# Sliding-window attention ahead of a routed network: the last half block of 64 keys goes into the fourth block's tile, padded with zeros to 128 rows

## The chip, the cores and the metric

The kernel runs on one core of one Trainium2 chip. The metric is device time in microseconds (us) of one execution; several executions are timed and the median is given. The five engines of the core are named as in the profile: PE (matrix multiplication; its loading of weights is listed apart as PEld), DVE (vector), ACT (scalar, activation functions), POOL (GpSimd) and SP, which here only issues DMAs. They run at the same time and wait for one another through semaphores; each works through its own list of instructions in order.

## What is computed

The first part is attention with a sliding window, for 8 batches, 8 heads, 576 positions and 64 values a head:

```python
scores = scale * np.matmul(q, k.transpose(0, 1, 3, 2))
rel = pos[:, None] - pos[None, :]
slopes = 2.0 ** (-8.0 * (np.arange(H) + 1) / H)
bias = slopes[:, None, None] * (-np.abs(rel))[None, :, :]
mask = (rel >= 0) & (rel < 128)
scores = np.where(mask, scores + bias[None], -1000000000.0)
attn = softmax(scores)            # over the keys
out = np.matmul(attn, v)
```

The outputs of the heads are put side by side into a token's 512 values, 4608 tokens in all. The second part is a network of 8 experts, every token through every expert:

```python
P = np.exp(x @ w_gate - max)
for _ in range(8):                # rows and columns in turn
    P /= P.sum(1, keepdims=True) + 1e-09
    P /= P.sum(0, keepdims=True) + 1e-09
    P *= N / E
for e in range(E):
    out += P[:, e:e+1] * (np.maximum(x @ w1[e], 0.0) @ w2[e])
```

The change lies in the attention alone.

## The kernel before

**Tiling of the attention.** A batch's 576 positions are cut into four blocks of 128 and a half block of 64 (`SM` = 512, `TL` = 64, `NKB` = 5 blocks). A query sees only keys of its own block and of the block before it. So a step `(b, kb, u)` takes batch `b`, key block `kb` and one half of the heads (`u` = 0 or 1, four heads each). Scores are made transposed, keys on the partitions and queries along the row, so that they can be the stationary operand of the product with v without another transpose.

- `scores` (L407) multiplies block `kb` of the keys with the queries of blocks `kb` and `kb + 1`. Each head has 64 values, so its operands lie on 64 partitions; two heads (`hb` = 0 and 1) lie on partitions 0 to 63 and 64 to 127 and are issued as a pair. Blocks 0 to 2 give 128 by 256 scores a head in one matmul (L416). Block 3 takes two: 128 queries of its own (L416) and the 64 of the half block (L423), 192 columns in all. Block 4 is the half block: 64 keys by 64 queries (L416).
- `exps` (L430) lets ACT take the exponential of the four heads' scores from PSUM into the tile `pt`; `masks` (L442) lets DVE multiply `pt` with a precomputed `mask`, which holds the position bias as a factor and zero outside the window. The mask of a head has 256 columns: own block, next block. `make_mask` (L237) has ACT write it once, at the start.
- `values` (L453) multiplies, for each head, `pt` of the block before and of the own block with v (65 columns: 64 values and a column of ones, which gives the sum of the weights) into one PSUM tile `psN`, eight matmuls of 128 by 128 by 65. For block 4 these are four matmuls with 128 rows and 64 columns, then four of 64 by 64 (L469 puts them in that order). DVE divides by the sums (L482, L483) into `xsb`.
- `turn_x` (L500) transposes `xsb` for the second part, through PE in batches 0 to 2 and 7 and through a DMA in batches 3 to 6, and stores it to DRAM through SP (`xd`, L498).

**The half block's q and k.** `load_tail` brings 64 rows of q and 64 of k of all heads; transposed, they stand in the tile `TT` (`homes`, L295), 64 columns of queries and 64 of keys. In batches 0 to 2 PE transposes them and ACT copies them there (L364), in later batches a DMA does it (`turn_tail`, L321). v comes in by `load_v`, and POOL casts it to 16 bits (`cast_v`, L384), with a small clearing that writes the column of ones (L389).

**The order of the work.** The program writes out each engine's order by hand (L693 to L798). In step n, the scores and exponentials of a later step are issued first, then a piece of filler, then the next step's mask, then the products with v of the step itself, then more filler. Filler is work of the second part that doesn't wait for the attention of this batch: the two layers of experts 0 and 1 on blocks that are done (`psh`, L117, and `psy`, L141, matmuls of 128 by 128 by 512). How many pieces each step gets is computed when the program is built, from constants for the cost of a piece and from how many are left; nothing in it depends on the scores. Batch 0 has no filler; short matmuls without use (`spin`, L253) stand between its steps.

**Loads.** SP issues nearly all DMAs in one queue, in order: q and k of batch `b + 2` are asked for in the middle of batch `b` (L771), v block by block. ACT casts k (L293), DVE casts q (L291), ahead of their transposes.

**Behind the attention** (L799 on) come the balancing of `P`, and then experts 2 to 7 with their matrices cut in quarters (L983, L1020). The change touches none of this.

Of the kernel before, what the change touches and what calls it, by code (L numbers as in the profile page):

```python
# [14 lines left out]
def kernel(  # L15
# [10 lines left out]
    nc = tc.nc  # L26
# [206 lines left out]
    if True:  # L233
        mask = asb.tile([P, H, 2 * P], FP16, name="mask")
        rel = per.tile([P, HD], FP16, name="rel", tag="yo", bufs=YO)[:, 0 : 2 * P]

        def make_mask(ys):  # L237
            for y in ys:
                nc.scalar.activation(
                    out=mask[:, y, :], in_=rel, func=AF.Exp, scale=-float(slopes[head_of[y]])  # L240
                )

# [78 lines left out]
        def turn_tail(b):  # L321
            t16 = asb.tile([P, HD], FP16, name=f"t16_{b}", tag="xsb", bufs=XSB)
            nc.gpsimd.tensor_copy(out=t16, in_=tails.pop(b).rearrange("p h d -> p (h d)"))
            nc.sync.dma_start(out=QKT[b][2], in_=t16, transpose=True)
# [21 lines left out]
        def turn_pe(b, kq, j):  # L346

            wide = j == NDT
            ps = aps.tile([P, RI, P], FP32 if wide else FP16, name=f"psT_{b}_{kq}_{j}", tag="pmm", bufs=4)
            for i in range(RI):  # L350
                if wide:
                    src = tails[b][:, 2 * i : 2 * i + 2, :]
                else:
                    src = c16s[b][:, kq, i, 2 * j : 2 * j + 2, :]
                nc.tensor.matmul(  # L355
                    out=ps[:, i, :],
                    lhsT=src.rearrange("p h d -> p (h d)"),
                    rhs=ident32 if wide else ident,
                    is_transpose=True,
                    start=(i == 0),  # L360
                    stop=(i == RI - 1),
                )
            if wide:
                nc.scalar.copy(out=QKT[b][2], in_=ps)  # L364
# [19 lines left out]
        def cast_v(m):  # L384
# [4 lines left out]
            nc.gpsimd.memset(vt[:, :, Dh : Dh + 2], 1.0)  # L389
# [8 lines left out]
        def sizes(kb):  # L398
            nk = P if kb < NKB - 1 else TL
            nn = 0 if kb == NKB - 1 else (P if kb < NKB - 2 else TL)  # L400
            return nk, nn
# [5 lines left out]
        def scores(b, kb, u):  # L407

            nk, nn = sizes(kb)
            ps = sps.tile([P, 2, 2, 2 * P], FP32, name=f"psS_{b}_{kb}_{u}", tag="psS", bufs=2)  # L410
            both = kb < NKB - 2
            for y in range(2):
                j = 2 * u + y
                for hb in range(2):
                    n = 2 * P if both else nk
                    nc.tensor.matmul(  # L416
                        out=ps[0:nk, hb, y, 0:n],
                        lhsT=cols(b, 1, j, hb, kb),
                        rhs=cols(b, 0, j, hb, kb, 1 + both),
                    )  # L420
                for hb in range(2):
                    if nn and not both:
                        nc.tensor.matmul(  # L423
                            out=ps[0:nk, hb, y, nk : nk + nn],
                            lhsT=cols(b, 1, j, hb, kb),
                            rhs=cols(b, 0, j, hb, kb + 1),
                        )
            pss[b, kb, u] = ps

        def exps(b, kb, u):  # L430
            nk, nn = sizes(kb)
            ps = pss.pop((b, kb, u))
            pt = asb.tile([P, 4, 2 * P], FP16, name=f"pt_{b}_{kb}_{u}", tag="pt", bufs=4)
            nc.scalar.activation(  # L434
                out=pt[0:nk, :, 0 : nk + nn],
                in_=ps[0:nk, :, :, 0 : nk + nn].rearrange("p a y n -> p (a y) n"),
                func=AF.Exp,
                scale=scale,
            )
            pts[b, kb, u] = pt  # L440

        def masks(b, kb, u):  # L442
            nk, nn = sizes(kb)
            pt = pts[b, kb, u]
            hs = slice(4 * u, 4 * u + 4)
            w = nk + nn
            nc.vector.tensor_tensor(  # L447
                out=pt[0:nk, :, 0:w], in0=pt[0:nk, :, 0:w], in1=mask[0:nk, hs, 0:w], op=ALU.mult
            )
# [3 lines left out]
        def values(b, kb, u):  # L453

            nk, _ = sizes(kb)
# [7 lines left out]
            for y in range(2):  # L463
                for hb in range(2):
                    hh = 2 * y + hb
                    if kb > 0:
                        ops.append((hh, pts[b, kb - 1, u][:, 2 * hb + y, P : P + nk], vs[b, kb - 1][:, 4 * u + hh, 0 : Dh + 1]))
                    ops.append((hh, pts[b, kb, u][0:nk, 2 * hb + y, 0:nk], vs[b, kb][0:nk, 4 * u + hh, 0 : Dh + 1]))
            if kb == NKB - 1:  # L469
                ops = ops[0::2] + ops[1::2]  # L470
            for i, (hh, lhsT, rhs) in enumerate(ops):
                nc.tensor.matmul(  # L472
                    out=psN[0:nk, hh, :],
# [26 lines left out]
        def turn_x(b, kb):  # L500
            nk, _ = sizes(kb)
# [165 lines left out]
        cast_v(3)  # L667
        cast_v(4)
        for j in (2, 3):
            cast_qk(1, j, (0,), True)  # L670
        load_weights(0, 1, 2)
# [3 lines left out]
        for j in range(2):  # L675
# [5 lines left out]
            turn_pe(0, 0, j)  # L681
        cast_qk(0, 2)
# [10 lines left out]
        for n, (b, kb, u) in enumerate(steps):  # L693
# [6 lines left out]
            if nxt:  # L700
# [548 lines left out]
```

## Time and profile before

| | |
|---|---|
| three executions | 1013.42, 1010.76 and 1014.03 us; median 1013.42 |
| the profiled execution | 1012.89 us |
| its span, first to last instruction | 1011.1 us |
| PE busy | 998.0 us (99%), 11583 matmuls |
| DVE busy | 758.4 us (75%) |
| ACT busy | 727.4 us (72%) |
| POOL busy | 79.2 us (8%) |
| PE's products with v in the attention (L472) | 576 matmuls, from 13.0 to 277.0 us |

A line of the trace in order of time reads: start in us, time it took, engine, line of the kernel, operation, written tile <- read tiles, shape, count of instructions that were merged, and in brackets how long the engine had been idle before it and what ended that. For a matmul the shape gives the stationary operand as rows*columns, then the moving operand. A grouped line gives the count, the busy time, the mean duration in nanoseconds, then the idle time before its instructions and what ended it. "q" behind an engine's name (SPq) is its queue of issued DMAs. Matmuls overlap one another, so the sum of their durations is more than the time they use.

### The profile page before, as it was taken

What the parts mean: (1) busy time and instruction counts of PE and PEld (TensorE: products, weight loads), DVE (VectorE), ACT (ScalarE), POOL (GpSimd) and SP (SyncE); (2) the same over time, 40 slices, a digit from 0 to 9 for tenths busy, and PEclk for the clock granted to TensorE, in tenths of its full rate; (3) what the DMA queues carried; (4) which work ended last, traced back from release to release, by engine and by line L of the source; (5) the groups of instructions that cost most, each with busy time, mean ns of one, the idle gap of its engine ahead of it and who ended that gap; (6) DMA issues with size and microseconds to landing.
All of it is one profiled execution on the core that took longest, in us unless ns stands there. A gap on an engine that the chain in (4) does not pass through costs nothing.

```text
span 1011.1 us, 27987 instructions
## 1 busy us (share of the span) xinstructions
PE 998.0 (99%) x11583; PEld 802.8 (79%) x11583; DVE 758.4 (75%) x1614; ACT 727.4 (72%) x1252; POOL 79.2 (8%) x143
## 2 busy tenths in 40 slices
PE   8999999999999999999999999999999999999998
PEld 5645444444544799999999999999999999999997
DVE  5737666655578989877877887887887787787787
ACT  7655554555333668888888888888888888888885
POOL 2312033315110000000000000000000000000000
PEclk9999999999999999999999999999999999999999
DMA  9997689888999334334333324335433333433361
GB/s 239 232 268 190 153 224 227 190 191 162 225 192 195 75 64 98 77 65 96 74 65 95 74 65 97 80 62 99 82 66 88 86 80 69 96 75 69 96 116 48
DMA packets 264431, 122.46 MB, mean 121 GB/s; under 512 B 201968, under 2 KB 255728, under 8 KB 264304
## 3 DMA queue, kind: packets, MB, share of 16 engines
q1 hardware_dynamic: 249568, 102.68, 44.8%
q0 software_dynamic: 14304, 17.84, 10.5%
q8 instruction: 90, 1.47, 0.6%
q14 instruction: 37, 0.30, 0.1%
q10 hardware_dynamic: 432, 0.16, 0.1%
HBM read 78.30 MB, written 23.59 MB: 101 GB/s over the span
## 4 chain that ended last, share of the span: by engine, by line
PE 92%; DVE 3%; DMA 2%; ACT 1%; issue 0%; SPq 0%; POOL 0%; DVEq 0%; ACTq 0%; POOLq 0%
PE psM L1020 31%; PE psB L983 14%; PE psh L117 12%; PE psy L141 11%; PE psA L983 9%; PE psC L983 9%; PE psN L472 2%; DMA k<-in_k_dram 2%; PE psS L416 2%; ACT pt L434 1%; PE psT L355 1%; PE psX L510 0%; DMA qk<-c 0%; DVE pt L447 0%; PE psh L962 0%
## 5 line engine op out<-in xcount | busy, mean ns | idle before, releaser
L1020 PEld LDWEIGHTS <-hs 128*128 128x128 f16 x2996 | 270.9, 98 | 22.6 <-DVE hs L1000 0.4
L1020 PE MATMUL psM<-w2l,hs 128*128 128x256 f16 x1440 | 186.7, 273 | 0.2 <-DVE hs L1000 0.2
L983 PEld LDWEIGHTS <-w1l 128*128 128x128 f16 x2848 | 181.3, 98 | 4.9 <-issue 0.5
L996 ACT ACTIVATE hs<-hs 128x512 f16<-128x512 f16 x212 | 130.2, 629 | 35.4 <-DVE hs L1166 25.8
L983 PEld LDWEIGHTS <-s 128*128 128x128 f16 x2136 | 141.6, 98 | 6.5
L1166 DVE TENSOR_TENSOR hs<-psB,s5y 128x512 f16<-128x512 f32 x106 | 73.3, 691 | 97.6 <-ACT xs L892 89.4
L117 PE MATMUL psh<-xT,w1t 128*128 128x512 f16 (+1 forms) x608 | 140.1, 372 | 0.4 <-ACT hT L129 0.4
L892 ACT ACTIVATE xs<-xtok,L_sb 128x512 f16<-128x512 f16 x204 | 136.3, 721 | 3.8 <-DMA xset<-xs 3.6
L129 ACT ACTIVATE hT<-psh 128x512 f16<-128x512 f32 (+1 forms) x144 | 83.3, 586 | 75.9 <-PE psh L117 75.8
L141 PE MATMUL psy<-w2t,hT 128*128 128x512 f16 x576 | 135.5, 380 | 0.0
L1020 PE MATMUL psM<-more,hs 128*128 128x256 f16 x864 | 129.5, 273 | 0.0
L983 PE MATMUL psB<-xset,s 128*128 128x128 f16 x1424 | 108.7, 219 | 0.0
L983 PE MATMUL psA<-xset,w1l 128*128 128x128 f16 x1424 | 108.6, 219 | 0.0
L141 PEld LDWEIGHTS <-hT 128*128 128x128 f16 x576 | 53.4, 98 | 59.6 <-issue 1.9
L434 ACT ACTIVATE pt<-psS 128x1024 f16<-128x1024 f32 (+2 forms) x80 | 67.6, 851 | 43.7 <-PE psS L416 20.3
L117 PEld LDWEIGHTS <-w1t 128*128 128x128 f16 x608 | 55.1, 99 | 53.3 <-issue 4.3
L559 DVE CAST yo<-psy 128x512 f16<-128x512 f32 x65 | 44.7, 691 | 61.6 <-PE psy L141 59.1
L1000 DVE TENSOR_TENSOR hs<-hs 128x1024 f16<-128x1024 f16 x107 | 73.9, 690 | 20.9 <-ACT hs L996 18.8
L1157 ACT COPY psC<-psB 128x512 f32<-128x512 f32 x106 | 60.4, 570 | 39.1 <-PE psB L983 39.1
L1149 ACT COPY s5y<-psC 128x512 f32<-128x512 f32 x106 | 62.1, 586 | 21.6 <-PE psC L983 21.5
L447 DVE TENSOR_TENSOR pt<-pt,mask 128x1024 f16<-128x1024 f16 (+2 forms) x80 | 52.4, 656 | 33.5 <-ACT pt L434 33.4
L1064 DVE TENSOR_TENSOR acc<-acc,psM 128x256 f32<-128x256 f32 (+1 forms) x162 | 73.9, 502 | 0.3
(122 smaller groups left out, 1400.1 us busy)
## 6 DMA issues: line engine op xcount, KB each, us to landing
s5y<-ysp SPq DMA_DIRECT2D x36, 256.0 KB, 3.0
ysp<-yo SPq DMA_DIRECT2D x65, 128.0 KB, 3.5
v<-in_v_dram SPq DMA_DIRECT2D x32, 256.0 KB, 4.2
out_dram<-acc SPq DMA_DIRECT2D x31, 256.0 KB, 2.5
q<-in_q_dram SPq DMA_DIRECT2D x5, 1024.0 KB, 7.7
k<-in_k_dram SPq DMA_DIRECT2D x5, 1024.0 KB, 9.4
xtok<-xd SPq DMA_DIRECT2D x34, 128.0 KB, 2.2
w2t<-in_moe_w_dram POOLq DMA_DIRECT2D x4, 1024.0 KB, 12.6
```

Of the source, the lines that this page charges most:

```text
L117: nc.tensor.matmul(out=ps[:, 0:nt], lhsT=w1ts[e][:, dt, P * ft : P * ft + P], rhs=xT[:, at : at + nb, dt, :], start=(dt == 0), stop=(dt == ...
L129: nc.scalar.activation(out=st["hT"][:, ft, 0:nt], in_=ps[:, 0:nt], func=AF.Relu)
L141: nc.tensor.matmul(out=ps, lhsT=st["hT"][:, ft, P * ms : P * ms + P], rhs=w2ts[e][:, ft, :], start=(ft == 0), stop=(ft == NFT - 1),)
L434: nc.scalar.activation(out=pt[0:nk, :, 0 : nk + nn], in_=ps[0:nk, :, :, 0 : nk + nn].rearrange("p a y n -> p (a y) n"), func=AF.Exp, scale ...
L892: nc.scalar.mul(out=xs[2 * (n % 2) + m], in_=xtok[m], mul=P_sb[:, blk, e : e + 1])
L983: nc.tensor.matmul(out=ps[:, j, :], lhsT=q[k][:, P * j : P * j + P], rhs=xset[n % 2][:, x, P * k : P * k + P], start=(start and j == 0 and ...
L996: nc.scalar.activation(out=h[n][:, slot], in_=src, func=AF.Relu)
L1000: nc.vector.tensor_tensor(out=t[:, 4:6], in0=t[:, 0:2], in1=t[:, 2:4], op=ALU.add)
L1020: nc.tensor.matmul(out=Ms[bk][:, half, :], lhsT=h[n][:, LEFT[m], f, :], rhs=W2L[e][RIGHT[m]][:, f, :], start=(e == 2 and f == 0 and half = ...
L1064: nc.vector.tensor_tensor(out=a, in0=a, in1=p2, op=op)
L1149: nc.scalar.copy(out=s5, in_=pc)
L1166: nc.vector.tensor_tensor(out=h[n][:, 3], in0=pb, in1=s5, op=ALU.add)
```

## The change

The half block's 64 by 64 scores are no longer a step of their own. They are made together with block 3, into the 64 columns of its tile that were free, and with 128 rows, the lower 64 of which come from zeros:

- `TT` grows from 128 to 192 columns, the last 64 cleared by POOL in `homes`. Columns 64 to 191 are then 128 "keys", 64 of them zeros.
- Block 3's tile holds, for each head: columns 0 to 63, padded half-block keys by half-block queries; columns 64 to 127, block 3's keys by half-block queries; columns 128 to 255, block 3's keys by its own queries. It is three matmuls a head in place of two, and block 4's one is gone.
- `exps` and `masks` always work on 128 by 4 by 256. Both are left out for block 4.
- The mask of a head grows from 256 to 384 columns. Blocks 0 to 2 use the last 256, block 3 the first 256; POOL makes the first 128 from the others at the start (`tail_masks`), ahead of the casts of v's blocks 3 and 4, of two casts of q and of the load of w2, which now stand behind it in the program.
- `cast_v` has POOL clear the lower 64 rows of the half block's v.
- `values` for block 4 multiplies columns 64 to 191 of block 3's tile with block 3's v and columns 0 to 127 with the padded v, 128 by 128 each. Rows 64 to 127 of the result are not used.

The core of the diff:

```diff
-        mask = asb.tile([P, H, 2 * P], FP16, name="mask")
+        mask = asb.tile([P, H, 3 * P], FP16, name="mask")
+        mask_of = {kb: mask[:, :, P : 3 * P] if kb < NKB - 2 else mask[:, :, 0 : 2 * P] for kb in range(NKB - 1)}
...
+        def tail_masks():
+
+            nc.gpsimd.memset(mask[TL:P, :, 0:TL], 0.0)
+            nc.gpsimd.tensor_copy(out=mask[0:TL, :, 0:TL], in_=mask[0:TL, :, P : P + TL])
+            nc.gpsimd.tensor_copy(out=mask[:, :, TL:P], in_=mask[:, :, 2 * P : 2 * P + TL])
...
-            TT = asb.tile([P, NDT, P], FP16, name=f"tT_{b}", tag="tT", bufs=2)
+            TT = asb.tile([P, NDT, P + TL], FP16, name=f"tT_{b}", tag="tT", bufs=2)
+            nc.gpsimd.memset(TT[:, :, P : P + TL], 0.0)
...
-            nc.gpsimd.memset(vt[:, :, Dh : Dh + 2], 1.0)
+            if nk < P:
+                nc.gpsimd.memset(vt[nk:P], 0.0)
+            nc.gpsimd.memset(vt[0:nk, :, Dh : Dh + 2], 1.0)
...
+                    tail_q = [cols(b, 0, j, hb, NKB - 1) for hb in range(2)]
+                    tail_k = [QKT[b][2][64 * hb : 64 * hb + 64, j, TL : TL + P] for hb in range(2)]
+                    own_k = [cols(b, 1, j, hb, kb) for hb in range(2)]
+                    parts = [
+                        (P, P, own_k, [cols(b, 0, j, hb, kb) for hb in range(2)]),
+                        (TL, TL, own_k, tail_q),
+                        (0, TL, tail_k, tail_q),
+                    ]
+                for at, n, ks, qs in parts:
+                    for hb in range(2):
+                        nc.tensor.matmul(out=ps[:, hb, y, at : at + n], lhsT=ks[hb], rhs=qs[hb])
...
-                        ops.append((hh, pts[b, kb - 1, u][:, 2 * hb + y, P : P + nk], vs[b, kb - 1][:, 4 * u + hh, 0 : Dh + 1]))
-                    ops.append((hh, pts[b, kb, u][0:nk, 2 * hb + y, 0:nk], vs[b, kb][0:nk, 4 * u + hh, 0 : Dh + 1]))
-            if kb == NKB - 1:
-                ops = ops[0::2] + ops[1::2]
+                        t, at = (pts[b, kb - 1, u], P) if kb < NKB - 1 else (pts[b, kb - 1, u], TL)
+                        ops.append((hh, t[:, 2 * hb + y, at : at + P], vs[b, kb - 1][:, 4 * u + hh, 0 : Dh + 1]))
+                    t, at = (pts[b, kb, u], P * (kb == NKB - 2)) if kb < NKB - 1 else (pts[b, kb - 1, u], 0)
+                    ops.append((hh, t[:, 2 * hb + y, at : at + P], vs[b, kb][:, 4 * u + hh, 0 : Dh + 1]))
...
-                elif nxt[2] == 0:
+                elif nxt[2] == 0 and nxt[1] < NKB - 1:
                     scores(*nxt)
                     scores(*nxt[:2], 1)
-                exps(*nxt)
+                if nxt[1] < NKB - 1:
+                    exps(*nxt)
             got = filler.fill(1.0) if b else 0.0
-            if nxt:
+            if nxt and nxt[1] < NKB - 1:
                 masks(*nxt)
```

The counts of instructions move so: ACT and DVE 16 fewer each, POOL 19 more, PE and SP the same.

More of the change, by code (lines that the diff above doesn't have):

```diff
@@ L363, in turn_pe @@
             if wide:
-                nc.scalar.copy(out=QKT[b][2], in_=ps)
+                nc.scalar.copy(out=QKT[b][2][:, :, 0:P], in_=ps)
                 return
@@ L407, in scores @@
         def scores(b, kb, u):
-            nk, nn = sizes(kb)
             ps = sps.tile([P, 2, 2, 2 * P], FP32, name=f"psS_{b}_{kb}_{u}", tag="psS", bufs=2)
-            both = kb < NKB - 2
             for y in range(2):
                 j = 2 * u + y
[L414 to L427, printed above, removed]
+                if kb < NKB - 2:
+                    parts = [(0, 2 * P, [cols(b, 1, j, hb, kb) for hb in range(2)], [cols(b, 0, j, hb, kb, 2) for hb in range(2)])]
+                else:
+                    tail_q = [cols(b, 0, j, hb, NKB - 1) for hb in range(2)]
[6 more added lines that the diff above has]
+                    ]
@@ L440, in exps @@
             pts[b, kb, u] = pt
         def masks(b, kb, u):
-            nk, nn = sizes(kb)
             pt = pts[b, kb, u]
[L445 to L449, printed above, removed]
+            nc.vector.tensor_tensor(out=pt, in0=pt, in1=mask_of[kb][:, 4 * u : 4 * u + 4, :], op=ALU.mult)
         xsbs: dict = {}
         def values(b, kb, u):
-            nk, _ = sizes(kb)
+            nk = sizes(kb)
@@ L500, in turn_x @@
         def turn_x(b, kb):
-            nk, _ = sizes(kb)
+            nk = sizes(kb)
             blk = 4 * b + kb if kb < NKB - 1 else 4 * B + b // 2
@@ L681 @@
             turn_pe(0, 0, j)
+        tail_masks()
+        cast_v(3)
+        cast_v(4)
+        for j in (2, 3):
+            cast_qk(1, j, (0,), True)
+        load_weights(0, 1, 2)
         cast_qk(0, 2)
```

23 lines of the change are left out of this document (5 added, 18 removed).

## The prediction

> **What bounds the kernel now.** I read the page's head first, then the busy time by stretch, then TensorE's own instructions in order of time around one batch.
>
> ```profile
> span 1011.1 us, 27987 instructions
> PE 998.0 (99%) x11583; PEld 802.8 (79%) x11583; DVE 758.4 (75%) x1614; ACT 727.4 (72%) x1252; POOL 79.2 (8%) x143
> ...
> 0.00:28.00 28.00, 23.29 (x252) 16.48 (x253) 15.61 (x39) 19.64 (x35) 5.36 (x17) 1.00 1.01 249
> 28.00:60.00 32.00, 30.44 (x308) 18.88 (x306) 20.17 (x51) 19.95 (x35) 7.43 (x17) 1.00 1.13 226
> 100.00:150.00 50.00, 47.78 (x361) 22.77 (x361) 31.63 (x74) 27.35 (x44) 11.07 (x21) 0.97 0.76 191
> 150.00:200.00 50.00, 50.00 (x407) 24.64 (x406) 31.41 (x69) 27.29 (x44) 15.95 (x24) 1.00 0.91 204
> 400.00:450.00 50.00, 50.00 (x682) 47.42 (x680) 40.98 (x84) 41.77 (x74) 0.00 (x0) 1.00 0.34 75
> ```
>
> The columns of the stretches are length, then busy time of PE, PEld, DVE, ACT and POOL, then granted clock, DMA share and GB/s. PE is busy without a break from 150 us on (50.00 of 50.00), while DVE and ACT have 18 us or more to spare in the attention stage and some 8 us behind it. Whatever PE no longer does in the attention stage should therefore come off the end, unless something makes PE wait instead. Only the first batch (0 to 28 us) and 100 to 150 us show PE waiting.
>
> Matmuls overlap, so their durations are no price. A price is the distance from a group's start to the next group's start. This is TensorE around the end of one batch:
>
> ```profile
> 163.60 1.89 PE L117 MATMUL psh<-xT,w1t 128*128 128x512 f16 x8
> 165.42 0.31 PE L416 MATMUL psS<-tT 64*64 64x64 f16 x8
> 165.66 1.04 PE L117 MATMUL psh<-xT,w1t 128*128 128x512 f16 x4
> 166.54 0.41 PE L472 MATMUL psN<-v,pt 128*128 128x65 f16 x8
> 166.78 1.89 PE L117 MATMUL psh<-xT,w1t 128*128 128x512 f16 x8
> 168.50 1.89 PE L141 MATMUL psy<-w2t,hT 128*128 128x512 f16 x8
> 170.32 0.56 PE L472 MATMUL psN<-v,pt 128*64 128x65 f16 x8
> 170.81 1.90 PE L141 MATMUL psy<-w2t,hT 128*128 128x512 f16 x8
> ```
>
> **The change, part by part.**
>
> *Products of the half block with v (16 groups: 8 batches, two halves of the heads).* Eight 128 by 128 products take 166.54 to 166.78 = 0.24 us. The half block's eight (four of 128 by 64, four of 64 by 64, merged into one row) take 170.32 to 170.81 = 0.49 us. A run of eight large matmuls takes 1.72 us ahead of another 128 by 128 group (166.78 to 168.50), but 1.82 us ahead of the half block's (168.50 to 170.32): 0.10 us of emptying before the shape changes. The change makes all eight 128 by 128, so each group should save 0.49 - 0.24 + 0.10 = 0.35 us, and 16 x 0.35 = 5.6 us. Bounds: 16 x 0.25 = 4.0 if the 0.10 stays for another reason, 5.6 if not.
>
> Here a rule speaks against the change. The Trainium skill, TensorEngine Tiling (Array Packing), Theoretical Speedup, says that operands of at most 64 rows or columns run up to twice as fast when packed as small tiles of the array than when they fill it. By that rule padding throws speed away. The rows above say the opposite for this order of instructions, since the narrow groups take twice as long, and I go by the rows.
>
> *Scores of the half block (8 times, both halves of the heads together).* The separate group goes: 165.42 to 165.66 = 0.24 us, and the run ahead of it takes 1.82 us (163.60 to 165.42) in place of 1.72, so 0.34 us a batch. The same number of matmuls comes back in the fourth block's group, now with 128 columns of keys, of which 64 are zeros:
>
> ```profile
> 158.34 0.23 PE L416 MATMUL psS<-qN,kN 64*128 64x128 f16 x2
> 158.41 0.19 PE L423 MATMUL psS<-tT,kN 64*128 64x64 f16 x2
> 158.43 0.22 PE L416 MATMUL psS<-qN,kN 64*128 64x128 f16 x2
> ...
> 158.78 1.04 PE L117 MATMUL psh<-xT,w1t 128*128 128x512 f16 x4
> ```
>
> A pair of that very shape (64 by 128 keys, 64 queries, L423) takes 158.41 to 158.43, about 0.03 us; four more pairs are 0.12 us. No row shows it with the same queries twice, so the bounds are 0.10 and the old 0.24. I take the near row: 0.34 - 0.12 = 0.22 a batch, 1.8 us over 8. PE in all: 5.6 + 1.8 = 7.4 us, bounds 4.0 + 0.8 and 5.6 + 2.0.
>
> *Exponentials and masks.* The fourth block's become 128x1024, the half block's disappear:
>
> ```profile
> L434 ACT ACTIVATE pt<-psS 128x1024 f16<-128x1024 f32 x48 | 48.8, 1026 | 18.0 <-PE psS L416 18.0
> L447 DVE TENSOR_TENSOR pt<-pt,mask 128x1024 f16<-128x1024 f16 x48 | 33.9, 705 | 25.8 <-ACT pt L434 25.8
> L447 DVE TENSOR_TENSOR pt<-pt,mask 128x768 f16<-128x768 f16 x16 | 13.9, 872 | 5.7 <-ACT pt L434 5.7
> L434 ACT ACTIVATE pt<-psS 128x768 f16<-128x768 f32 x16 | 12.8, 808 | 20.9 <-PE psS L423 20.0 <-PE psN L472 0.7
> L434 ACT ACTIVATE pt<-psS 64x256 f16<-64x256 f32 x16 | 5.9, 370 | 4.8 <-PE psN L472 2.6 <-PE psS L416 2.2
> L389 POOL MEMSET v<- 128x16 f16 x40 | 6.2, 156 | 0.0
> L388 POOL CAST v<-v 64x512 f16<-64x512 f32 x8 | 5.1, 632 | 19.4 <-DMA v<-in_v_dram 11.0 <-PE psh L117 8.4
> L447 DVE TENSOR_TENSOR pt<-pt,mask 64x256 f16<-64x256 f16 x16 | 4.6, 290 | 2.0 <-ACT pt L434 1.9
> ```
>
> ACT saves 808 + 370 - 1026 = 152 ns, DVE 872 + 290 - 705 = 457 ns, each 16 times. Neither bounds the stage, so I count this at nothing. The cover is PE's filler (the large matmuls between steps). Batch 0 has no filler, and batch 1 has little. There the fourth block's exponentials, 0.22 us longer each, end later, and PE waits for their masks:
>
> ```profile
> 21.06 0.94 DVE L447 TENSOR_TENSOR pt<-pt,mask 128x768 f16<-128x768 f16 x1
> 22.06 0.39 PE L472 MATMUL psN<-v,pt 128*128 128x65 f16 x7 [0.77 <-DVE pt L447]
> 22.47 0.55 DVE L447 TENSOR_TENSOR pt<-pt,mask 128x768 f16<-128x768 f16 x1
> ```
>
> What is late next in batches 0 and 1 is the mask of the fourth block's second half, since PE gets there a quarter microsecond sooner, the scores in between being gone. I give back 0.3 us in each, bounds 0 and 0.4: 0.6 us.
>
> *POOL.* It gets 19 more instructions: 8 clearings of the keys' padding (128x256), 8 of v's (64x528), 3 that extend the mask. Between the 0.16 of a small clearing and the 0.63 of the 64x512 cast above, that is 3 to 12 us on an engine busy 79 of 1011 us. The three mask instructions are placed where POOL stands idle:
>
> ```profile
> 16.09 0.74 POOL L666 DMA_DIRECT2D wg_sb<-in_moe_w_gate_dram  x1
> 20.98 0.61 POOL L388 CAST v<-v 128x512 f16<-128x512 f32 x1 [4.15 <-DMA v<-in_v_dram]
> ```
>
> About 2 us of work fits in 4.15, and the casts and the load of w2 queued behind them keep their time; the fourth block's first mask, which newly waits for POOL, comes only at 21.06. But POOL at work slows DVE: that mask took 0.94 us beside the cast, the next one of the same size 0.55. One slowed mask in batch 0 costs 0 to 0.39; I take 0.3. Without the idle 4.15 us the load of w2 would come 2 us later.
>
> *SP's queue.* No DMA is added or moved; the transposing DMA of a tail writes rows 192 apart in place of 128, nothing in my sum. But its loads decide the two places where this stage already waits at a change of batch:
>
> ```profile
> 103.76 0.62 ACT L293 CAST c<-k 128x512 f16<-128x512 f32 x1 [3.65 <-DMA k<-in_k_dram]
> 106.80 0.68 SPq L498 DMA_DIRECT2D xd<-xsb  x1
> 109.57 1.02 PE L117 MATMUL psh<-xT,w1t 128*128 128x512 f16 x4 [0.42 <-ACT hT L129]
> 113.96 1.22 SPq L523 DMA_TRANSPOSE xT<-xsb  x1
> 130.87 0.58 SPq L275 DMA_DIRECT2D k<-in_k_dram  x1
> 139.22 0.62 ACT L293 CAST c<-k 128x512 f16<-128x512 f32 x1 [7.39 <-DMA k<-in_k_dram]
> 141.54 0.30 PE L472 MATMUL psN<-v,pt 128*128 128x65 f16 x4 [1.73 <-DVE pt L447]
> ...
> 141.60:147.90 6.30, 6.23 (x35) 2.65 (x36) 4.27 (x11) 3.95 (x7) 1.09 (x4) 0.73 0.55 155
> ```
>
> The load of k issued at 130.87 lands at 139.22; behind its cast on ACT stand the next batch's exponentials, then masks on DVE, then PE. SP issued nothing from 107.48 to 113.96, when a transposed block that PE's side had to finish came up, so the load moves up with the earlier batches' gain; but PE gains another 0.35 x 2 + 0.22 = 0.92 us within the batch, and that much can turn into waiting, here and at 109.57. Two places, 0 to 0.92 each; I take half: 0.9 us.
>
> **The sum.** -7.4 + 0.6 + 0.3 + 0.9 = -5.6 us. The profiled execution took 1012.89 us (span 1011.1), 0.53 below the median of 1013.42. So 1012.89 - 5.6 = 1007.3 us. The terms' ends give -(7.6 - 0) and -(4.8 - 0.8 - 0.4 - 1.8): 1005.3 to 1011.1.
>
> **The rivals.**
>
> *PE's gain is eaten by waiting (no change).* For it: in the first 60 us the DMA share is above 1, and two changes of batch wait for a load already. Against it: SP idles 6 us before 113.96, and from 150 us on PE never waits. If nothing of batches 0 to 3 comes through, 4 x 0.92 = 3.7 us remain: 1009.2; with one more microsecond lost at a later change of batch, about 1010.5.
>
> *The late load becomes a stall at more changes of batch (slower).* The stall at 141.54 costs 1.73 us of idling, and after it the granted clock is 0.73 for 6.3 us, 27% of which is 1.7: 3.4 us. ACT waits for k also at 103.76, and by smaller amounts at the next two changes of batch. If these three became such stalls, 10.2 us come back: 1017.5. It decides from two on (6.8 against 5.6), and needs each load later than its slack. For it: the waits exist. Against it: PE closes in by 0.92 us only.
>
> *The stall goes.* Should that load of k land 2 us earlier beside the shifted traffic, idle time and lowered clock both go: 1007.3 - 3.4 - 0.5 = 1003.4.
>
> *Narrow is faster.* If the padded groups took twice the narrow ones' 0.49 us, 16 x 0.49 = 7.8 us would be added, less 1.8: 1018.9. This is what the rule of the skill's tiling page comes to; 166.54 to 166.78 speaks against it.
>
> **How the numbers follow.** The sum as reckoned has 62 in 100, the stall that goes 10, the gain eaten 16, more stalls 11, narrow faster 1. A change under 0.3% (3 us) cannot be told from none here. So faster 0.72, same 0.16, slower 0.12. The range takes in the sum's ends, the stall that goes and the eaten gain: 1003.2 to 1012.8; the likeliest case alone is 1005.3 to 1011.1.
>
> **What would show it.** Right: every product group with v starts 0.24 us before the next group, runs ahead of them at 1.72; no 64x64 forms of the scores and of the products with v; the fourth block's scores 0.56 in place of 0.44 us; attention ends about 5.6 us sooner, and the stretch behind it is as long as before. Wrong: a PE wait above 2.7 us near 140 us, a granted clock below 1 in a second place, waits of PE for masks after batch 1, or masks of 128x1024 above 0.8 us because their mask operand is now three blocks wide.

## The result and the profile after

The changed kernel takes 1008.93 us (median of 21 executions, 1006.29 to 1013.57); the kernel before, in as many executions, 1012.86 us (1009.68 to 1014.08). The ratio is 0.9966, 95% interval 0.9956 to 0.9976: faster by 3.4 us, interval 2.4 to 4.5 (the medians alone differ by 3.9). A second set of executions gave 1009.53 us and 0.9955 (0.9938 to 0.9972). The forecast was 5.6 us less, so about 2.2 us are missing. The two profiled executions of the change, 1013.57 and 1013.39 us, are at the slow end of its range, so what is said below on batches goes by several profiles.

The page of the changed kernel: busy time of each engine, then its instructions grouped by form.

```profile
PE 992.8 (98%) x11583; PEld 802.5 (79%) x11583; DVE 755.6 (75%) x1598; ACT 726.7 (72%) x1236; POOL 92.7 (9%) x162
...
L439 ACT ACTIVATE pt<-psS 128x1024 f16<-128x1024 f32 x64 | 65.1, 1025 | 37.7 <-PE psS L433 37.3 <-PE psN L467 0.4
L444 DVE TENSOR_TENSOR pt<-pt,mask 128x1024 f16<-128x1024 f16 x64 | 47.8, 747 | 34.2 <-ACT pt L439 34.2
L467 PE MATMUL psN<-v,pt 128*128 128x65 f16 x576 | 32.2, 194 | 9.3 <-DVE pt L444 6.1 <-POOL v L399 3.2
```

All 64 exponentials and masks and all 576 products now have one form each. PE is busy 5.2 us less (998.0 before), POOL 13.5 us more. The last row also shows PE waiting 3.2 us for POOL, which writes v (L399); in this execution the kernel before has no such wait.

The changed kernel's PE in order of time, first the fourth block's scores with the padded half block's in between, then the end of a batch:

```profile
125.64 1.46 PE L141 MATMUL psy<-w2t,hT 128*128 128x512 f16 x6
127.03 0.23 PE L433 MATMUL psS<-qN,kN 64*128 64x128 f16 x2
127.09 0.19 PE L433 MATMUL psS<-tT,kN 64*128 64x64 f16 x2
127.12 0.19 PE L433 MATMUL psS<-tT 64*128 64x64 f16 x2
...
127.59 1.04 PE L117 MATMUL psh<-xT,w1t 128*128 128x512 f16 x4
...
170.10 0.41 PE L467 MATMUL psN<-v,pt 128*128 128x65 f16 x8
170.34 1.89 PE L117 MATMUL psh<-xT,w1t 128*128 128x512 f16 x8
172.07 1.89 PE L141 MATMUL psy<-w2t,hT 128*128 128x512 f16 x8
173.79 0.41 PE L467 MATMUL psN<-v,pt 128*128 128x65 f16 x8
174.04 1.24 PE L141 MATMUL psy<-w2t,hT 128*128 128x512 f16 x5
```

The fourth block's group takes 127.03 to 127.59 = 0.56 us. The half block's product group takes 173.79 to 174.04 = 0.25, and the run of eight ahead of it 172.07 to 173.79 = 1.72. These are the predicted figures: TensorE's prices hold. The gain is lost elsewhere.

Where it is lost can be read by batch. Each figure is the distance in us between the first products with v of one batch and the next (the last batch: to its last product); "behind" is the rest of the span. The lower rows are experiments told below.

| kernel | 0 | 1 | 2 | 3 | 4 | 5 | 6 | 7 | behind |
|---|---|---|---|---|---|---|---|---|---|
| before | 23.3 | 41.3 | 30.2 | 33.9 | 35.7 | 33.8 | 33.8 | 32.2 | 734.1 |
| changed | 23.9 | 43.6 | 29.4 | 35.1 | 34.7 | 32.9 | 32.9 | 31.4 | 734.5 |
| changed, again | 25.8 | 41.1 | 29.3 | 34.8 | 35.8 | 32.9 | 33.3 | 31.4 | 734.3 |
| narrow products | 23.6 | 41.2 | 30.0 | 34.3 | 35.3 | 33.5 | 33.5 | 32.0 | 734.3 |
| more PE work in batch 0 | 23.5 | 40.8 | 29.3 | 34.6 | 35.6 | 32.8 | 33.0 | 35.9 | 734.2 |
| more PE work in batch 5 | 23.6 | 40.7 | 29.5 | 34.5 | 34.6 | 35.8 | 32.8 | 31.4 | 734.2 |
| batch 3 turned by PE | 25.1 | 40.7 | 29.4 | 32.1 | 33.4 | 32.9 | 33.3 | 31.4 | 734.2 |
| the same on before | 25.7 | 41.7 | 30.2 | 33.0 | 34.1 | 33.8 | 33.8 | 32.2 | 734.4 |
| turned by PE, padding first | 22.7 | 40.9 | 29.4 | 32.1 | 34.0 | 32.9 | 32.9 | 31.4 | 734.2 |

Batches 2, 5, 6 and 7 are shorter by 0.8 to 0.9 us (batch 6 of the repeated profile by 0.5). Batches 3 and 4 together took 69.6 us before and 69.7 and 70.6 after: nothing gained. Batches 0 and 1 differ by more from one execution to the next than by the change.

At the change from batch 3 to 4 the changed kernel's timeline (SPq is SP's queue of issued DMAs) shows the same chain as before, later and longer:

```profile
133.70 0.83 SPq L282 DMA_DIRECT2D k<-in_k_dram  x1
...
143.13 0.62 ACT L300 CAST c<-k 128x512 f16<-128x512 f32 x1 [9.07 <-DMA k<-in_k_dram]
143.66 1.02 ACT L439 ACTIVATE pt<-psS 128x1024 f16<-128x1024 f32 x1
...
144.71 0.69 DVE L444 TENSOR_TENSOR pt<-pt,mask 128x1024 f16<-128x1024 f16 x1 [3.50 <-ACT pt L439]
...
145.46 0.30 PE L467 MATMUL psN<-v,pt 128*128 128x65 f16 x4 [3.74 <-DVE pt L444]
```

The load of k for batch 5 is issued at 133.70 and cast at 143.13: 9.4 us, against 8.3 before (130.87 to 139.22). Behind the cast on ACT stands the exponential of batch 4, then its mask, then PE, which idles 3.74 us instead of 1.73. Three other profiles of this code with padded products (the repeated one and those with more PE work) have 2.92, 3.26 and 2.73 us there, the one with narrow products 2.40. The clock that was granted afterwards is in the changed kernel's stretches (busy time of PE, PEld, DVE, ACT and POOL, clock, DMA share, GB/s):

```profile
42.40:48.00 5.60, 5.59 (x62) 3.67 (x62) 2.34 (x7) 1.97 (x3) 5.27 (x12) 0.70 0.84 159
...
145.40:151.00 5.60, 5.47 (x30) 2.34 (x31) 4.37 (x12) 3.37 (x6) 2.34 (x5) 0.70 0.53 153
151.00:157.00 6.00, 6.00 (x48) 2.94 (x47) 2.42 (x6) 5.49 (x10) 1.45 (x3) 1.00 1.11 176
```

From 145.4 on it is 0.70 on average over 5.6 us; read in steps of half a microsecond it is 0.50 from 146.1 to 149.5 and 1.00 before and behind. In this execution the same happened once more, after 42.4; the chain there is another:

```profile
41.31 0.98 POOL L396 CAST v<-v 128x512 f16<-128x512 f32 x1 [7.75 <-DMA v<-in_v_dram]
42.24 0.11 POOL L399 MEMSET v<- 128x16 f16 x1
...
42.41 0.37 PE L467 MATMUL psN<-v,pt 128*128 128x65 f16 x7 [2.63 <-POOL v L399]
```

A load of v came late in batch 1, and PE stood 2.63 us. The repeated profile has no such wait there (0.96), but one of 2.48 us in batch 0, for the same reason.

### The profile page after: what moved, and what is told of

Same layout as the page of the kernel before. It is cut to its first block, busy times and chain, and to the rows that moved or that the text cites. A ratio compares the mean times of both kernels' runs of the same rounds, so it can differ in the third digit from the quotient of the medians.

```text
span 1011.8 us, 27964 instructions
## 1 busy us (share of the span) xinstructions
PE 992.8 (98%) x11583; PEld 802.5 (79%) x11583; DVE 755.6 (75%) x1598; ACT 726.7 (72%) x1236; POOL 92.7 (9%) x162
## 4 chain that ended last, share of the span: by engine, by line
PE 87%; DMA 5%; DVE 2%; issue 2%; SPq 1%; ACT 1%; POOL 1%; POOLq 0%; DVEq 0%; ACTq 0%
PE psM L1017 30%; PE psB L980 13%; PE psy L141 11%; PE psh L117 10%; PE psA L980 9%; PE psC L980 9%; DMA v<-in_v_dram 2%; DMA q<-in_q_dram 1%; DMA k<-in_k_dram 1%; PE psN L467 1%; PE psS L433 1%; DMA xset<-xs 1%; SPq L386 1%; POOL kN L324 0%; PE psh L959 0%
## 5 line engine op out<-in xcount | busy, mean ns | idle before, releaser
L1017 PEld LDWEIGHTS <-hs 128*128 128x128 f16 x2996 | 271.1, 98 | 22.6 <-DVE hs L997 0.4
L439 ACT ACTIVATE pt<-psS 128x1024 f16<-128x1024 f32 x64 | 65.1, 1025 | 37.7 <-PE psS L433 37.3
L1142 ACT COPY psB<-psA 128x512 f32<-128x512 f32 x106 | 60.8, 573 | 17.9 <-PE psA L980 17.8
```

The lines of the kernel that those rows point to most:

```text
L439: nc.scalar.activation(out=pt, in_=ps.rearrange("p a y n -> p (a y) n"), func=AF.Exp, scale=scale)
L1017: nc.tensor.matmul(out=Ms[bk][:, half, :], lhsT=h[n][:, LEFT[m], f, :], rhs=W2L[e][RIGHT[m]][:, f, :], start=(e == 2 and f == 0 and half = ...
```

## The experiments

Each ratio is to executions of the kernel before on the same chip.

**The half block's products narrow again, all else as changed.**

```diff
-ops.append((hh, t[:, 2 * hb + y, at : at + P], vs[b, kb - 1][:, 4 * u + hh, 0 : Dh + 1]))
+ops.append((hh, t[:, 2 * hb + y, at : at + nk], vs[b, kb - 1][:, 4 * u + hh, 0 : Dh + 1]))
...
-ops.append((hh, t[:, 2 * hb + y, at : at + P], vs[b, kb][:, 4 * u + hh, 0 : Dh + 1]))
+ops.append((hh, t[0:nk, 2 * hb + y, at : at + nk], vs[b, kb][0:nk, 4 * u + hh, 0 : Dh + 1]))
+if kb == NKB - 1:
+    ops = ops[0::2] + ops[1::2]
...
-out=psN[:, hh, :],
+out=psN[0:nk, hh, :],
```

> The changed kernel, but the half block's products with v are 64 columns wide again (four of 128 by 64, then four of 64 by 64), all else as changed. Theory A (TensorE's price of 0.35 us a group holds, but what is gained in batches 0 to 3 is lost again to waiting for loads): the eight groups of batches 4 to 7 come back, 2.8 us on top of the changed kernel, so 0.6 to 1.1 us below the kernel before. Theory B (the price holds everywhere and something else in the change costs about 2 us): all 16 groups come back, 5.6 us, so 1.7 to 2.2 us above the kernel before.

Measured: 1012.9 us, 0.9998 (0.9988 to 1.0008). Making the products narrow again takes back 3.2 us, about 1.4 to either side: within the noise, all that the change gains. PE at the end of a batch in this kernel:

```profile
168.01 1.89 PE L141 MATMUL psy<-w2t,hT 128*128 128x512 f16 x8
169.83 0.56 PE L469 MATMUL psN<-v,pt 128*64 128x65 f16 x8
170.32 1.90 PE L141 MATMUL psy<-w2t,hT 128*128 128x512 f16 x8
```

The narrow group takes 0.49 us and the run ahead of it 1.82, as in the kernel before, so both belong to the shape and not to the place. In batches 2, 5, 6 and 7 the narrow kernel is 0.6 to 0.7 us longer than the changed one (0.70 was priced for two groups) and about 0.2 shorter than before (the scores, priced at 0.22). The rise of 3.2 us is nearer to the theory by which only some batches hand the gain on than to the full 5.6.

The weight loads of this same kernel, grouped by form, and then the loads of one narrow group in order of time:

```profile
L469 PEld LDWEIGHTS <-pt 128*128 128x128 f16 x448 | 21.9, 98 | 21.0 <-DVE pt L444 8.8 <-issue 1.0
L469 PEld LDWEIGHTS <-pt 64*64 64x64 f16 x64 | 3.3, 106 | 0.9 <-issue 0.3
L469 PEld LDWEIGHTS <-pt 128*64 128x64 f16 x64 | 3.2, 110 | 6.4 <-issue 5.5 <-DVE w2l L631 0.4 <-DVE rden L479 0.4
...
169.83 0.44 PEld L469 LDWEIGHTS <-pt 128*64 128x64 f16 x8 [0.42 <-issue]
```

The same in the changed kernel:

```profile
173.58 0.49 PEld L467 LDWEIGHTS <-pt 128*128 128x128 f16 x8
```

A load of 64 columns takes 106 to 110 ns, one of 128 columns 98. The Trainium skill, TensorE: Matmul & The Clock Gate, Weight-path perf modes, says that the fast way of loading weights is taken when the operand has 128 columns and isn't 32-bit; by that rule 64 columns go the slow way. The rows agree: 64 columns are no quicker to load than 128. A run that takes the fast way from the 128 columns was not made.

The slower loads are the smaller part of the price, though. Most of it is paid where the stationary operand changes its shape. The starts of single matmuls between 152 and 275 us show it. Among 128 by 128 products the next starts 30 ns later, among narrow ones of one shape 40 ns (means). But the first narrow product starts 309 ns behind the last large matmul, where a 128 by 128 product starts after 216; the step from 128 by 64 to 64 by 64 takes 123 ns in place of 30, and so does the step to the large matmul behind. These are three times about 93 ns, 0.28 us of the 0.34 us that a narrow group costs more; the 10 ns more at each of the other six steps are the rest. The two rows above show the same from the loads' side. The padded group's first load starts at 173.58, 0.21 us ahead of its matmul at 173.79. The narrow group's starts at 169.83, together with its matmul, after 0.42 us without a load. The padded group pays none of the three steps because its shape is that of the matmuls around it.

**PE work added where nothing else is changed.** Three more short matmuls without use ahead of each product group of one batch, 3.3 us of PE in all, once in batch 0 and once in batch 5.

```diff
             if b == 0:
-                spin(psN, 3)
+                spin(psN, 6)
```

> The changed kernel with three more useless matmuls ahead of each of the ten product groups of batch 0, 10 x 0.33 = 3.3 us of TensorE. Theory A (loads pace the first batches): within 1 us of the changed kernel, 2.5 to 4 us below the kernel before. Theory B (TensorE paces them): 3.3 us above the changed kernel, within 1 us of the kernel before.

```diff
             if b == 0:
                 spin(psN, 3)
+            if b == 5:
+                spin(psN, 3)
```

> The changed kernel with the same 3.3 us of useless matmuls in batch 5 in place of batch 0. Both theories: TensorE paces batch 5, so 3.3 us above the changed kernel, within 1 us of the kernel before. A smaller rise would mean that TensorE's time is not what counts there either.

Measured: in batch 0, 1011.59 us, 0.9979 (0.9961 to 0.9996); in batch 5, 1011.41 us, 0.9982 (0.9969 to 0.9996). The ratios do not tell the two apart, and by them the work in batch 0 does not stay within 1 us of the changed kernel's 0.9966. The lowest of the twelve times differ: 1005.20 us with the work in batch 0, below every execution of the changed kernel, and 1008.86 with it in batch 5. So do the batches (table above). Batch 5 grew by 2.9 us. Batch 0 did not grow: 23.5 us, against 23.6 in the kernel with the work in batch 5, whose batch 0 is that of the changed kernel. PE in batch 0 with the added work:

```profile
22.96 0.82 PE L260 MATMUL psN<-ones 128*128 128x256 f16 x6
23.61 0.19 PE L467 MATMUL psN<-v,pt 128*128 128x65 f16 x1
23.98 0.37 PE L467 MATMUL psN<-v,pt 128*128 128x65 f16 x7 [0.18 <-POOL v L399]
```

The added work went into waits that PE has there anyway: 0.18 us is left where the changed kernel has 0.55, and over the whole batch PE idles 1.0 us instead of 3.4. It is one profile each, and batch 0 of the same code varies by more than 2 us; but by these PE's time does not set the length of batch 0, so shorter matmuls could not shorten it. The profile of this kernel has a wait of 2.92 us in batch 7 for a transposing DMA, which no other profile has and batch 0 does not explain.

**The loads of q and k asked for two steps sooner in every batch.**

```diff
-            if 1 <= b < B - 2 and at == 3:
+            if 1 <= b < B - 2 and at == 1:
                 load_qk(b + 2)
```

> The changed kernel with the loads of q and k for the batch after next asked for two steps sooner (after step 1 instead of step 3, ahead of the transposing DMAs). Theory A: the wait of TensorE at the change from batch 3 to 4 (3.74 us in the changed kernel's profile) shrinks below 1 us and the lowered clock behind it goes; 3 to 5 us below the changed kernel, 6 to 9 below the kernel before. Theory B: no wait of that kind matters in the mean, so within 1 us of the changed kernel.

Measured: 1020.45 us, 1.0071 (1.0055 to 1.0087), 10 us worse than the changed kernel. The theory that these loads are merely asked for too late fell. PE in this kernel waits at new places. The longest wait is in batch 1, 3.82 us at 70.67 for a cast of q on POOL; batch 1 takes 46.4 us and batch 5 37.6. Around the change from batch 3 to 4:

```profile
138.66 0.41 PE L467 MATMUL psN<-v,pt 128*128 128x65 f16 x8
138.99 0.28 PE L433 MATMUL psS<-qN,kN 64*128 64x256 f16 x2
140.21 0.28 PE L433 MATMUL psS<-qN,kN 64*128 64x256 f16 x2 [0.93 <-POOL kN L324]
141.58 0.28 PE L433 MATMUL psS<-qN,kN 64*128 64x256 f16 x2 [1.09 <-POOL kN L324]
142.58 0.28 PE L433 MATMUL psS<-qN,kN 64*128 64x256 f16 x2 [0.72 <-POOL kN L324]
```

Here k of the next batch, transposed by a DMA and then copied by POOL, comes too late for its scores.

**Only the load for batch 5, one step sooner, on both kernels.**

```diff
-            if 1 <= b < B - 2 and at == 3:
+            if 1 <= b < B - 2 and at == (2 if b == 3 else 3):
```

> The changed kernel with only the loads of q and k for batch 5 asked for one step sooner (in batch 3, behind the transposing DMAs and loads of the tail, ahead of the store, the load of v and the transpose that now stand in front of them on SP). Theory A (the wait at the change from batch 3 to 4 takes part of the gain): the wait of 2.7 to 3.7 us falls by 2 us or more, batch 3 goes from 34.5 us or more towards 33; 2 to 4 us below the changed kernel, 5 to 8 below the kernel before. Theory B (that wait is moved, not paid, by a later load): batch 3 gets shorter and a later batch longer by as much, within 1 us of the changed kernel.

> The kernel before with the same load one step sooner. Theory A: its wait at that place was 1.73 us with a lowered clock behind it, so 1.5 to 3.4 us below the kernel before, and the distance between this and the changed kernel with the same edit grows to 4 to 5 us. Theory B: within 1 us of the kernel before.

Measured: on the changed kernel 1011.04 us, 0.9976 (0.9965 to 0.9987); on the kernel before 1015.3 us, 1.0026 (1.0016 to 1.0036). On the kernel before that is 2.6 us worse than without the edit, which neither theory had; on the changed kernel it is no better (0.9976 against 0.9955 and 0.9966, with intervals that overlap). The changed kernel with it, in order of time:

```profile
134.64 0.62 ACT L300 CAST c<-k 128x512 f16<-128x512 f32 x1 [4.89 <-DMA k<-in_k_dram]
...
140.34 1.19 SPq L518 DMA_TRANSPOSE xT<-xsb  x1
...
142.75 1.89 PE L117 MATMUL psh<-xT,w1t 128*128 128x512 f16 x4 [4.68 <-DMA xT<-xsb]
```

k now comes in time: the cast starts at 134.64. But the transposing DMAs of batch 3's output, behind the load in SP's queue, come late, and PE waits 4.68 us for `xT`. The wait was moved, not removed. Against the changed kernel's first profile batch 3 became 3.9 us shorter (31.2) and batch 4 longer by 5.5 (40.2). The kernel before with the edit has a wait for `xT` of 3.31 us at the same place.

**That, and v's padding written before the cast that waits for v.** In the changed kernel POOL clears the padding behind the cast, and PE's 0.55 us at 25.49 (`POOL v L399`) ends with it.

```diff
-            nc.gpsimd.tensor_copy(out=vt[0:nk, :, 0:Dh], in_=v32s.pop((b, kb))[0:nk])
             if nk < P:
                 nc.gpsimd.memset(vt[nk:P], 0.0)
             nc.gpsimd.memset(vt[0:nk, :, Dh : Dh + 2], 1.0)
+            nc.gpsimd.tensor_copy(out=vt[0:nk, :, 0:Dh], in_=v32s.pop((b, kb))[0:nk])
```

> The changed kernel with the sooner load and with the clearing of v's padding (and the column of ones) ahead of the cast of v in place of behind it, so that it runs while POOL waits for the load. Theory A: the wait of TensorE for POOL at the end of batch 0 (0.55 to 0.83 us) goes, but batch 0 is paced by loads, so the time is that of the sooner load alone within 0.5 us. Theory B (that wait is part of what was lost): 0.5 to 1 us below the sooner load alone.

Measured: 1010.92 us, 0.9986 (0.9972 to 0.9999). No wait for POOL at 24 or 25 us is left in its profile, and batch 0 takes 23.1 us, against 23.2 without this edit. By these two profiles the wait had not lengthened the batch.

**The changed kernel once more**, beside the last three.

> The changed kernel itself, on the same chip as the three above: 3 to 4.5 us below the kernel before; batch 5 and 6 take 32.9 us each by the trace, 0.9 less than before, and batch 0 no less than before.

Measured: 1009.53 us, 0.9955 (0.9938 to 0.9972), 4.6 us below the kernel before. In its profile (table above) batch 5 takes 32.9 us as expected, batch 6 33.3 and batch 0 25.8.

**The output of batch 3 transposed by PE instead of by DMAs, on both kernels.** This removes DMAs in place of moving them, at about 1.1 us of PE work by the estimate below.

```diff
         def by_pe(b):
-            return b < XPE or b == B - 1
+            return b <= XPE or b == B - 1
```

> The changed kernel, with the output of batch 3 transposed by PE and no longer by DMAs (five groups of PE, about 5 x 0.22 = 1.1 us more PE work in batch 3, five transposing DMAs fewer before its end). Theory A: what is lost between batch 3 and batch 4 is lost to traffic: the load of k for batch 5 and the transposing DMAs of batch 3 share the same time, and the fewer of them there are, the sooner the load lands. Then the wait of PE at the change from batch 3 to 4 (2.6 to 3.7 us in the changed kernel) falls below 1 us, the lowered clock behind it goes, batches 3 and 4 together (69.8 us) come to 67 to 68.5, and the time is 1.5 to 3 us below the changed kernel, at 0.994 to 0.995 of the kernel before. Theory B: the load takes as long by itself as it takes beside them; the wait stays above 2 us, and the time is 0 to 1.5 us above the changed kernel, at 0.997 to 0.998.

> The same edit alone on the kernel before. Theory A: its wait of 1.73 us at 141.54 and the lowered clock behind it go, against 1.1 us more PE work: 1 to 2.5 us faster, 0.9975 to 0.999. Theory B: wait and clock stay, and it is 1 us slower: 1.000 to 1.002. If the gain here is the same as on the changed kernel, the change had brought no wait of its own; if it is smaller here, the difference is what the change lost there.

Measured: on the changed kernel 1006.02 us (1005.15 to 1007.82), 0.9934 (0.992 to 0.9947); on the kernel before 1011.25 us (1009.86 to 1013.57), 0.9986 (0.9974 to 0.9998). The changed kernel with the edit, in order of time, and its clock in the stretches where the changed kernel had 0.70:

```profile
124.77 1.72 SPq L282 DMA_DIRECT2D k<-in_k_dram  x1
...
135.35 0.62 ACT L300 CAST c<-k 128x512 f16<-128x512 f32 x1 [2.14 <-DMA ysp<-yo]
...
140.92 0.29 PE L467 MATMUL psN<-v,pt 128*128 128x65 f16 x4
```

```profile
139.90:145.00 5.10, 4.85 (x39) 2.36 (x38) 5.00 (x14) 2.38 (x4) 2.26 (x6) 1.00 0.36 100
145.00:151.00 6.00, 6.00 (x48) 2.92 (x47) 2.60 (x7) 5.33 (x9) 0.00 (x0) 1.00 0.66 152
```

SP reaches the load of k 16.0 us after the start of batch 3 (124.77, start 108.8) instead of 23.3 (133.70, start 110.4): two transposing DMAs that stood ahead of it in the queue, at 116.69 and 129.10 in the changed kernel, are gone. The load itself is no shorter. It lands 10.6 us after its issue, against 9.4 in the changed kernel; on the kernel before it is 10.2 us with the edit and 8.3 without. The cast still starts as soon as it lands (the row names another DMA, but the load landed at 135.33), and that is 6 us sooner within the batch. Batch 4's first product at 140.92 waits for nothing, and the clock stays at 1.00. So theory A's forecast holds, but not its reason: with the transposing DMAs gone the load is not faster, it is issued sooner, and this time nothing else stands behind it too late.

On the changed kernel the edit brings 3.2 us (0.9966 to 0.9934), on the kernel before 1.4. With the edit on both sides the change is worth 0.9934 / 0.9986 = 0.9948, or 5.3 us, close to the 5.6 forecast. The intervals leave about 2 us to either side, so the 1.8 us between 3.2 and 1.4 are not settled by the times alone. Batches 3 and 4 in the profiles point the same way: without the edit they take 69.6 us in the kernel before and 69.9 in the changed one (mean of four), with it 67.1 and 65.5 (66.1 in the next experiment).

**Both, on the changed kernel:** batch 3 by PE and the padding first, two edits shown above.

> The same edit on the changed kernel, and v's padding and column of ones written before the cast that waits for v's load instead of behind it. Theory A: as x3_by_pe within 0.5 us, or up to 0.7 us faster for the waits of PE for POOL at 25 us. Theory B of this point: the loads pace batch 0 and 1 whatever POOL does, and it is as x3_by_pe within 0.5 us to both sides.

Measured: 1004.89 us (1004.06 to 1006.44), 0.9925 (0.9913 to 0.9938). It is the fastest version, ahead of both kernels. Its 0.9 us over the last one are within the intervals; what the padding's place adds stays open.

## Why the prediction was right, and where it was off

The time lies in the range, 1.6 us above the forecast, and faster was the right side. That it still lies in the range is in part luck: two terms were mis-sized, and the width of the range covered them. By its own steps:

- *Products of the half block with v* (5.6 us, 0.35 a group): the rows give 0.24 to 0.25 and 1.72, and undoing them costs 0.6 to 0.7 us a batch where PE sets the pace, against 0.70. Right. What the prediction took for slow narrow matmuls with some emptying ahead is mostly three changes of shape a group. The rule of the Trainium skill, TensorEngine Tiling (Array Packing), Theoretical Speedup, which the prediction set against the change, speaks of small operands packed as tiles; these groups issue theirs one after another, and narrow was slower by 3.2 us. No run here packs them.
- *Scores of the half block* (0.22 a batch): the group takes 0.56, and about 0.2 us a batch remain in the narrow kernel. Right.
- *Exponentials and masks at nothing*: right from batch 2 on, where PE waits for masks at the same two places as before (0.36 us in batch 2, as before, and at the change from 3 to 4). But a sign named as wrong did appear, masks above 0.8 us: the fourth block's masks average 0.87. The mask's three blocks are not the cause. These rows are DVE's and POOL's in the changed kernel:

```profile
128.53 0.69 DVE L444 TENSOR_TENSOR pt<-pt,mask 128x1024 f16<-128x1024 f16 x1 [0.70 <-ACT pt L439]
...
196.12 4.57 POOL L324 COPY kN<-qk 128x512 f16<-128x512 f16 x4 [9.56 <-DMA qk<-c]
196.49 1.24 DVE L444 TENSOR_TENSOR pt<-pt,mask 128x1024 f16<-128x1024 f16 x1 [0.70 <-ACT pt L439]
```

Both are masks of the fourth block. The first has no work of POOL beside it (POOL's copies start at 129.31) and takes 0.69, the other 1.24. Of the fourth block's 16 masks, 6 run alone and take 0.68 to 0.69; the other 10 run beside POOL and take 0.99 on average. Not every one is slowed: one that started together with a copy, at 131.31, took 0.69, and the copy 1.61. The Trainium skill, SBUF — State Buffer, Who interferes with whom, says that a vector instruction with two inputs in SBUF contends with a GpSimd instruction that reads SBUF. These rows agree. In the kernel before the fourth block's masks, 128x768, took the same 0.87 on average, again with 10 of 16 beside POOL. The prediction had set that mean against the 705 ns of masks that mostly run alone. So the saving on DVE was 52.4 to 47.8 us, 4.6 where 16 x 0.457 = 7.3 was reckoned. PE waits for masks at no new place.

- *Batches 0 and 1* (1.84 less, 0.9 given back for masks and POOL): this term was mis-sized. Five profiles whose first two batches run the changed code give 63.9 to 67.5 us, mean 65.7; three of the code before give 64.5 to 67.4, mean 65.9. So 0.2 instead of 0.94, within a spread of about 3 us that goes largely with when v lands (the wait of 2.63 us shown above is one such case). Masks and POOL were the wrong reason: PE work added to batch 0 left its length alone, and so did taking POOL's wait away in the kernel with the sooner load. In the kernel with batch 3 by PE, batch 0 went from 25.1 to 22.7 with the padding first; but the kernel before has 23.3 and 25.7 without any padding, so this pair does not tell. The prediction had the DMA share above 1 before its eyes and used it only for the rival. (The three batches of the code before are those of the kernel before and of its two edits, 64.5, 65.7 and 67.4.)
- *The two load waits* (0.9 us in sum, half of 0.92 each): mis-sized too. The one at 109.57 stayed (0.42 to 0.43). The one at 141.54 grew from 1.73 to between 2.73 and 3.74. Two things went otherwise than assumed. SP issued the load hardly sooner within the batch: 23.3 us after its start in the profile shown and 22.3 to 22.6 in the three others, against 23.2 before. And the load took longer: 9.4 to 10.1 us in the four profiles with padded products, 8.3 before and 8.4 with narrow ones. That length is not the change's alone, for with its two edits the kernel before has 9.3 and 10.2. Batches 3 and 4 were to give 0.92 and cost 0.3 (mean 69.9 against 69.6).
- *POOL at 3 to 12 us more*: 13.5, above the bound, since its casts of v became slower too (128x512: mean 790 ns, 706 before); PE does not wait for it from batch 2 on.
- *The stretch behind, as long as before*: 734.2 to 734.5 against 734.1.

By batch the account is: 0 and 1 -0.2, 3 and 4 +0.3, the other four -3.4, behind +0.2, together -3.1, to a measured -3.4. Of the rivals, "the gain is eaten by waiting" is the one that came partly true. Its 3.7 us from four batches is about what came through, though from batches 2, 5, 6 and 7. The sign named for a wrong forecast, a wait above 2.7 us near 140, came; a lowered clock at a second place came in both profiles of the change, in batch 0 or 1, but the kernel before with batch 3 by PE has a wait of 2.06 us and the clock lowered there too, so it comes without the change as well. More stalls at changes of batch did not come.

The mean granted clock that is on record for each execution says how often it was lowered. Of 27 executions of the changed kernel 8 are at 1.000 (mean 1006.8 us), 13 at 0.998 (1009.3) and 6 at 0.997 or less (1012.9). One stretch of 3.4 us at half clock takes the mean to 0.998. Of 72 executions of the kernel before, beside the experiments on three chips, 26 are at 1.000 (1011.8), 8 at 0.999, 33 at 0.998 (1013.6) and 5 at 0.997 or less (1015.8). Compared at the same clock the change is thus worth 4.9 us (1.000) and 4.3 us (0.998). By these counts a part of the missing 2.2 us is that a larger share of the changed kernel's executions have a lowered clock for longer than one such stretch, 6 of 27 against 5 of 72; that the change causes this is not shown. No profile was taken of the changed kernel at 1.000, so whether the wait near 141 exists there is open.

Why the load takes 8.3 us in one profile and 10.6 in another isn't settled. That it shares its time with the transposing DMAs is not what the runs show, since it took 9.6 to 10.6 us in the three profiles without them. What they show is the order of the queue: the load issued one step sooner made `xT` late, and with the transposes ahead of it taken out neither was late.

## What to carry to other kernels

A padded operand can be cheaper than a narrow one where it has the shape of the matmuls around it: read in the trace what the narrow group costs, together with the steps into and out of its shape, and not what share of the array it fills. Price the gain batch by batch and give nothing for those that a load paces; a wait for a load that already exists takes the whole gain ahead of it and can take more. Such a wait is not mended by asking sooner for the load when the queue is full: something else becomes late. What helped here was to take out transfers that stood ahead of it.

## What the runs showed of the hardware

A stationary operand of 64 columns took longer to load (106 to 110 ns) than one of 128 (98 ns). A change of the stationary operand's shape between two matmuls cost about 93 ns each time (309 against 216 ns, 123 against 30). Behind the first 20 us, most idle times of PE of 1.7 us and more came with a granted clock of 0.50, from late in the wait or from shortly behind it: for 3.4 us in the kernel before (143.0 to 146.4) and in the changed one (146.1 to 149.5), for 6.8 us in its repeated profile (143.4 to 150.2). The 0.70 to 0.73 of the stretches are means that take in some time at full clock. Another case is the 1.83 us wait in batch 0 of the kernel with batch 3 turned by PE:

```profile
24.05 0.37 PE L467 MATMUL psN<-v,pt 128*128 128x65 f16 x7 [1.83 <-POOL v L399]
```

```profile
24.00:30.00 6.00, 5.95 (x61) 5.06 (x61) 2.69 (x8) 1.91 (x4) 2.37 (x7) 0.72 1.15 333
```

It does not come each time: behind a wait of 2.62 us in batch 1 of the kernel before with the sooner load (until 40.49) the clock stayed at 1.00, and so it did behind waits of 0.96, 1.33 and 1.40 us in batches 0 and 1 of other profiles. Where it comes, 3.4 us at half clock are 1.7 us lost: the wait of 1.73 us cost about twice its length, that of 3.74 about one and a half times.
